# Windowed attention into a gated feed-forward layer: the output layer of five wide tiles as seven block products

## The chip, the cores and the metric

The kernel runs on one core of a Trainium2 chip. A core has a matrix engine (TensorE, PE in the profile), a vector engine (VectorE, DVE), a scalar engine (ScalarE, ACT), a general engine (GpSimd, POOL) and a queue engine (SyncE, SP) that issues transfers. Each engine works off its own instructions in order; semaphores tie them together. The metric is the device time of one execution in microseconds, the median of several runs.

## The reference

Eight batches of eight heads, 576 tokens each, head size 64: causal attention with a window of 64 tokens, then a gated feed-forward layer over all 4608 tokens (model width 512, inner width 1536).

```python
scores = (1.0 / np.sqrt(D)) * np.matmul(q, k.transpose(0, 1, 3, 2))
rel = pos[:, None] - pos[None, :]
scores = np.where((rel >= 0) & (rel < 64), scores, -1000000000.0)
attn = np.exp(scores - max) ; attn = attn / (sum + 1e-09)
x = np.matmul(attn, v)                    # (8, 8, 576, 64) -> (4608, 512)
gate = np.maximum(x @ w_gate, 0.0)        # (4608, 1536)
out = gate * (x @ w_val) @ w_out          # (4608, 512)
```

## The kernel before

**Tiles.** The tokens are cut into four narrow tiles of 384 and six wide tiles of 512. For the wide tiles (here "wide tile 1" to "wide tile 6"; `t` from 4 to 9 in the code) the work of one tile is: attention of the tile, a transposed and normalized input `xt` of 128 partitions by 4 by 512, the inner layer `fast_hidden` (L547), and the output layer `fast_output` (L646). The inner features are 12 blocks of 128.

**The inner layer.** It runs in three groups of two lower and two upper feature blocks. In each group the gate half is four plain products of `xt` with `wg` (L582), passed through a rectifier by ScalarE (L586) into `r4`. The value half is already done as seven block products for eight (Winograd's form of Strassen's method): the products P1, P6, P2, P5, P7, P4, P3 (L573, four matmuls of 256 columns each) use differences of the tokens (`xc`, made by `x_form` on DVE, L459) and differences of the weights (`vs`, made once by `w_form` on POOL, L480). Three running sums in a PSUM bank are copied out by ScalarE (`snap`, L593); DVE adds them to another bank (`vsum`, L600); POOL multiplies such a sum with the rectified gate into `g_sb` (L606). One quarter of a group needs no sum, and DVE multiplies it straight from the bank (L613). So per group there are three sums on DVE, three multiplications on POOL and one on DVE. P3 adds onto the bank that the second sum reads, and therefore comes after it.

**The output layer.** `fast_output` takes the tile's four quarters of 128 tokens in turn: 12 matmuls of 512 columns (L658) with a block of `g_sb` as the stationary operand and `wo` as the moving one, a copy to `o_sb` by ScalarE (L663) and a store of 128 rows by SP's queue (L665). In the last tile the last quarter goes out in three pieces of 256, 128 and 128 columns (`output_last`, L703 to L707).

**What stands between the quarters.** The attention of later tiles is worked into the output layer: `values` of the next tile (L422, 64 small matmuls for each half of the heads) before quarters one and two, `scores` of the tile after that (L253, 64 small matmuls) before quarters three and four. `values` needs three PSUM banks, which DVE's normalizations give back (`t_norm`, L441); `scores` needs four, which ScalarE's exponentials give back (L389). DVE then masks (L394), and `t_turn` (L447) transposes the result into `xt`.

**POOL's queue.** Besides its multiplications POOL issues the loads of queries, keys and values (L173, L199) and copies value rows between partition halves (L208, L210). A query or key load waits until DVE has transposed the batch that is in the buffer (L193).

**The order.** The program is written out by hand. A small planner (`Weaver`) keeps a clock that runs with the matmuls' modelled time and a heap of actions with due times; before each product the actions that are due are written into their engines' streams. What it settles is only the order in each engine; waits come from the data. Eight PSUM banks go round in a list `free`. A pool `g_sb` has two buffers, `r4` two, `vsum` four, `snap` five, `o_sb` three.

## Time and profile before

| | |
|---|---|
| median of 3 runs | 322.14 us (321.91 to 322.75) |
| the profiled execution's own time | 322.06 us |
| its span in the trace | 320.2 us |
| granted clock, mean | 0.995 |
| wide tiles 1 to 6 begin about (first product of the tile) | 122.3, 157.0, 190.0, 223.1, 256.0, 287.4 us |

The profile is of one execution. Times inside it are microseconds from the start of its span. A group's row gives line, engine, operation, output and inputs, shapes and count, then busy time and the mean of one in nanoseconds, then the idle time of the engine just ahead of these instructions and what ended it. A row of the chain or of an engine's instructions in order of time gives start, length, and what ran; "x8" means eight of them merged. Matmuls overlap in the pipeline, so the distance between starts is what one costs, not its own length.

### The profile page before, as it was taken

The numbers are of one execution on the slowest core, as the hardware profiler recorded it, in microseconds if no ns is written. First come the engines' busy times: TensorE is split into PE (matmuls) and PEld (weight loads), VectorE is DVE, ScalarE is ACT, GpSimd is POOL, SyncE is SP. The second block draws the span as 40 slices with busy tenths as digits, with TensorE's granted clock in tenths as the row PEclk, the third lists the DMA queues.
The fourth block names the chain that finished last, engine by engine and source line by source line (L and its number), as shares of the span: only waits on it lengthen the run. The fifth ranks groups of instructions, "written<-read, shape, count | busy, mean of one in ns | idle before, by whom it ended". The sixth has DMA issues, their size and how long they took to land.

```text
span 320.2 us, 9481 instructions
## 1 busy us (share of the span) xinstructions
PE 308.8 (96%) x4077; PEld 190.1 (59%) x4077; DVE 203.2 (63%) x397; ACT 158.1 (49%) x310; POOL 177.8 (56%) x206
## 2 busy tenths in 40 slices
PE   4799999999899999999999999999999999999996
PEld 2586958655546555665566556655665566546654
DVE  6937962667993996779576857686337734643420
ACT  3644325533524616752765276627652666326632
POOL 8859336215988506799168925980495036404540
PEclk9889999999999999999999999999999999999999
DMA  8999998946299149806910691039001100020002
GB/s 218 183 196 205 194 120 161 171 98 99 30 174 165 21 90 160 57 1 104 219 36 0 97 220 43 2 50 127 35 0 34 69 34 3 2 98 35 0 33 102
DMA packets 52491, 29.52 MB, mean 92 GB/s; under 512 B 38880, under 2 KB 43872, under 8 KB 52448
## 3 DMA queue, kind: packets, MB, share of 16 engines
q0 software_dynamic: 46688, 18.29, 49.3%
q1 hardware_dynamic: 5616, 10.55, 9.3%
q8 instruction: 32, 0.52, 0.7%
q14 instruction: 11, 0.09, 0.1%
q10 hardware_dynamic: 144, 0.07, 0.1%
HBM read 37.75 MB, written 9.44 MB: 147 GB/s over the span
## 4 chain that ended last, share of the span: by engine, by line
PE 89%; DVE 3%; ACT 2%; POOL 2%; DMA 2%; issue 1%; DVEq 0%; POOLq 0%
PE bank L658 19%; PE bank L582 19%; PE bank L538 17%; PE bank L573 17%; PE bank L673 10%; PE bank L253 3%; PE bank L422 2%; DVE p L292 2%; DMA v<-in_v_dram 2%; ACT pw L389 1%; PE bank L311 1%; DVE g_sb L525 1%; PE bank L703 1%; POOL v L199 1%; DVE qT L193 0%
## 5 line engine op out<-in xcount | busy, mean ns | idle before, releaser
L606 POOL TENSOR_TENSOR g_sb<-r,vsum 128x512 f16<-128x512 f32 x54 | 68.1, 1276 | 77.7 <-DVE vsum L600 75.7
L600 DVE TENSOR_TENSOR vsum<-bank,snap 128x512 f32<-128x512 f32 x54 | 37.3, 691 | 60.1 <-PE bank L573 36.5
L582 PE MATMUL bank<-xt,wg 128*128 128x512 f16 x288 | 73.9, 379 | 0.0
L658 PE MATMUL bank<-wo,g_sb 128*128 128x512 f16 x276 | 62.9, 380 | 0.0
L586 ACT ACTIVATE r<-bank 128x512 f32<-128x512 f32 x72 | 43.2, 600 | 32.3 <-PE bank L582 32.3
L658 PEld LDWEIGHTS <-g_sb 128*128 128x128 f16 x276 | 25.5, 98 | 28.9
L582 PEld LDWEIGHTS <-wg 128*128 128x128 f16 x288 | 28.2, 98 | 18.6
L525 DVE TENSOR_TENSOR g_sb<-r,bank 128x384 f16<-128x384 f32 x48 | 25.9, 550 | 20.3 <-PE bank L538 18.8
L522 ACT ACTIVATE r<-bank 128x384 f32<-128x384 f32 x48 | 23.7, 496 | 29.4 <-PE bank L538 20.3
L573 PEld LDWEIGHTS <-vs 128*128 128x128 f16 x288 | 28.0, 98 | 15.6 <-issue 1.6
L538 PE MATMUL bank<-xt,wg 128*128 128x192 f16 (+1 forms) x256 | 36.5, 296 | 0.5 <-DVE g_sb L525 0.4
L663 ACT COPY o_sb<-bank 128x512 f32<-128x512 f32 x23 | 13.5, 586 | 45.2 <-PE bank L658 43.2
L593 ACT COPY snap<-bank 128x512 f32<-128x512 f32 x54 | 31.6, 586 | 8.4 <-PE bank L573 8.4
L199 POOL DMA_DIRECT2D v<-in_v_dram x41 | 34.7, 865 | 1.8 <-DMA q<-in_q_dram 1.0
L538 PE MATMUL bank<-xt,wv 128*128 128x192 f16 (+1 forms) x256 | 34.3, 286 | 0.0
L673 PE MATMUL bank<-wo,g_sb 128*128 128x512 f16 x144 | 32.8, 379 | 0.2 <-DVE g_sb L525 0.2
L538 PEld LDWEIGHTS <-wg 128*128 128x128 f16 x256 | 24.3, 102 | 9.8 <-issue 0.9
L573 PE MATMUL bank<-xc,vs 128*128 128x256 f16 x216 | 29.4, 272 | 0.4 <-ACT snap L593 0.4
L208 POOL COPY v<-v 64x512 f16<-64x512 f16 (+1 forms) x22 | 16.1, 732 | 23.7 <-DMA v<-in_v_dram 22.6
L538 PEld LDWEIGHTS <-wv 128*128 128x128 f16 x256 | 22.9, 98 | 8.1
L394 DVE TENSOR_TENSOR pw<-pw,mask 128x512 f16<-128x512 f16 x48 | 20.2, 437 | 11.2 <-ACT pw L389 10.5
L389 ACT ACTIVATE pw<-bank 128x512 f16<-128x512 f32 x48 | 25.9, 608 | 1.5 <-PE bank L253 1.0
(69 smaller groups left out, 358.6 us busy)
## 6 DMA issues: line engine op xcount, KB each, us to landing
out_dram<-o_sb SPq DMA_DIRECT2D x35, 256.0 KB, 3.0
k<-in_k_dram POOLq DMA_DIRECT2D x15, 288.0 KB, 5.3
q<-in_q_dram POOLq DMA_DIRECT2D x15, 288.0 KB, 7.3
v<-in_v_dram POOLq DMA_DIRECT2D x31, 128.0 KB, 8.0
wg<-in_moe_w_gate_dram POOLq DMA_DIRECT2D x6, 256.0 KB, 6.4
wv<-in_moe_w_val_dram POOLq DMA_DIRECT2D x6, 256.0 KB, 8.2
wo<-in_moe_w_out_dram POOLq DMA_DIRECT2D x3, 512.0 KB, 11.9
v<-in_v_dram POOLq DMA_DIRECT2D x10, 64.0 KB, 5.9
```

Source lines behind the costliest of these rows:

```text
L199: nc.gpsimd.dma_start(v16s[b % 2][lo:hi, g, :, 0:64], v[b, :, 64 * g - 64 + lo:64 * g - 64 + hi].rearrange("h p d -> p h d"))
L389: nc.scalar.activation(d["p"][g].rearrange("p n c -> p (n c)"), d["st"][g], ACT.Exp, scale=scale)
L525: nc.vector.tensor_tensor(g_sb[:, f:f + w, c0:c0 + n], part(r_sb), part(h2), MUL)
L538: nc.tensor.matmul(h[:, b * n:b * n + n], wt[:, c, (f + b) * 128:(f + b) * 128 + 128], xt[:, c, c0:c0 + n], start=(c == 0), stop=(c == NC ...
L573: nc.tensor.matmul(at[to][:, HT * i:HT * i + HT], w[:, k, 128 * i:128 * i + 128], x[:, k], start=(first and i == 0 and k == 0), stop=(k == ...
L582: nc.tensor.matmul(to, wg[:, k, 128 * ff:128 * ff + 128], xt[:, k], start=(k == 0), stop=(k == NC - 1))
L586: nc.scalar.activation(r4[:, n], to, ACT.Relu)
L593: nc.scalar.copy(at[name], at["A"])
L600: nc.vector.tensor_tensor(v, at[to], at[name], ADD)
L606: nc.gpsimd.tensor_tensor(gh[:, 2 * j + HF * n:2 * j + HF * n + 2, h], rh[:, 2 * n:2 * n + 2, h], pair(v), MUL)
L658: nc.tensor.matmul(op, g_sb[:, f, 128 * sub:128 * sub + 128], wo[:, f], start=(i == 0), stop=(i == NF - 1))
L673: nc.tensor.matmul(op, g_sb[:, f, bass.ds(sub * 128, 128)], wo[:, f], start=(f == 0), stop=(f == NF - 1))
```

## The change

**The output layer of wide tiles 1 to 5** (`block_output`, in place of `fast_output`) becomes seven block products. The tile's `g_sb` is cut in two ways: lower and upper six feature blocks, first and second 256 tokens. The output weights are cut in lower and upper feature blocks and left and right 256 columns. Each product has 6 feature blocks by 2 token quarters, 12 matmuls of 256 columns, 84 in all where there were 48 of 512. The order is P1, P5, P6, half of P2, P7, the other half of P2, P4, P3, with `values` and `scores` at four places between. Three snapshots by ScalarE, three sums by DVE straight into `o_sb`, and one copy by ScalarE give the four quarters of the result, each 256 tokens by 256 columns. Wide tile 6 keeps the old form.

**The differences.** `wo_form` makes the weight differences `ws` once, 12 operations of 128 by 512 on POOL: six due at 50.5 us and after by the planner's clock, six due in the last narrow tile. `g_form` makes the token differences `s_sb` for each group of each of the five tiles: two on DVE (n = 0, 1) and two on POOL (n = 2, 3). They read what the group's multiplications wrote, so each stands behind these. In the third group of a tile one of POOL's three multiplications (lower features, first tokens) moves to DVE.

**POOL's order.** In wide tile 1 the six later weight differences stand behind the query loads: five ahead of the value loads, one behind them, all ahead of the first multiplication. In wide tiles 1 and 2 the key and query loads of a later batch stand in the third group between the first difference and the second multiplication.

**Even and odd tokens.** A window's 64 query tokens are split as even and odd in place of first and second 32 in `t_pv`, with strided weight loads, and the even ones fill the first half of the tile. A store then goes to every second row of `out`. With block products a store takes two pieces of 256 numbers per partition, in place of one of 512.

**Buffers.** `s_sb` shares the two-buffer pool of `g_sb`. The zeros that the early heating matmuls read lie in `ws` before it is used. The last tile's three last pieces use `o_sb` in place of own buffers.

```diff
@@ t_pv
-                    n = 2 * (QW * qh + i) + s
+                    n = 2 * QW * s + QW * qh + i
...
-                                         quads[qd]["p"][j][:, QW * hh + i, 32 * s:32 * s + 32],
+                                         quads[qd]["p"][j][:, QW * hh + i, s:64:2],
@@ after w_form
+    def wo_form(n, j):
+        f1, f2 = slice(HF + 2 * j, HF + 2 * j + 2), slice(2 * j, 2 * j + 2)
+        c1, c2 = slice(0, DM // 2), slice(DM // 2, DM)
+        b11, b12, b21, b22 = wo[:, f1, c1], wo[:, f1, c2], wo[:, f2, c1], wo[:, f2, c2]
+        to = ws[:, :, 2 * j:2 * j + 2]
+        x, y = ((b12, b11), (b22, to[:, 0]), (b22, b12), (b21, to[:, 1]))[n]
+        nc.gpsimd.tensor_tensor(to[:, n], x, y, SUB)
...
+    def g_form(t, n, j, eng):
...
+        a11, a12, a21, a22 = g_sb[:, f1, h1], g_sb[:, f2, h1], g_sb[:, f1, h2], g_sb[:, f2, h2]
...
+        x, y, op = ((a21, a22, ADD), (to[:, 0], a11, SUB), (a11, a21, SUB), (a12, to[:, 1], SUB))[n]
+        eng.tensor_tensor(to[:, n], x, y, op)
@@ fast_hidden, group
+                    late = t < LAST and j == NF // 4 - 1 and (n, h) == (0, 0)
...
-                        nc.gpsimd.tensor_tensor(gh[...], rh[...], pair(v), MUL)
+                        (nc.vector if late else nc.gpsimd).tensor_tensor(gh[...], rh[...], pair(v), MUL)
...
+            if t < LAST:
+                late = j == NF // 4 - 1
+                W.at(T + 6.2, lambda: g_form(t, 2, j, nc.gpsimd))
+                W.at(T + (7.1 if late else 9.0), lambda: g_form(t, 0, j, nc.vector))
+                W.at(T + (7.2 if late else 9.1), lambda: g_form(t, 1, j, nc.vector))
+                W.at(T + 8.8, lambda: g_form(t, 3, j, nc.gpsimd))
@@ new: block_output
+        forms = {"P1": (g_sb[:, f1, h1], wo[:, f1, c1], [(HF, 1)]), "P2": (g_sb[:, f2, h1], wo[:, f2, c1], [(0, 1)]),
+                 "P3": (s_sb[:, 3], wo[:, f2, c2], ["s", 3]), "P4": (g_sb[:, f2, h2], ws[:, 3], [(0, 0)]),
+                 "P5": (s_sb[:, 0], ws[:, 0], ["s", 0]), "P6": (s_sb[:, 1], ws[:, 1], ["s", 1]),
+                 "P7": (s_sb[:, 2], ws[:, 2], ["s", 2])}
...
+        run(0)
+        product("P1", "A", True)
+        snap("a1")
+        product("P5", "C", True)
+        run(1)
+        product("P6", "A", False)
+        snap("u2")
+        product("P2", "B", True, (0,))
+        run(2)
+        product("P7", "A", False)
+        snap("u3")
+        add(0.9, "C", "u3", False, 0, c2)
+        product("P2", "B", False, (1,))
+        add(0.1, "B", "a1", True, 1, c1)
+        product("P4", "A", False)
+        W.at(W.clock, direct)
+        run(3)
+        while ("summed", "u3") not in at:
+            W.pop()
+        product("P3", "C", False)
+        add(0.1, "C", "u2", True, 1, c2)
@@ output_last
-            o_sb = consts.tile([128, c1 - c0], FP32, name=f"o_last{c0}")
+            o_sb = f_sb.tile([128, DM], FP32, name="o_sb")[:, 0:c1 - c0]
@@ the plan
+        for j in range(NF // 4):
+            for n in range(2):
+                W.at(50.5 + 1.2 * (2 * j + n), lambda n=n, j=j: wo_form(n, j))
...
+                for j in range(NF // 4):
+                    for n in range(2, 4):
+                        W.at(T + 15.0 + 1.2 * (2 * j + n), lambda n=n, j=j: wo_form(n, j))
...
-                fast_output(t, between)
+                block_output(t, between)
```

## The prediction

> **What bounds the kernel now.** I read the page first (busy shares and the chain), then the groups, then one stretch per wide tile, then the queues of TensorE (PE), GpSimd (POOL) and VectorE (DVE) instruction by instruction. Page:
>
> ```profile
> PE 308.8 (96%) x4077; PEld 190.1 (59%) x4077; DVE 203.2 (63%) x397; ACT 158.1 (49%) x310; POOL 177.8 (56%) x206
> ...
> PE 89%; DVE 3%; ACT 2%; POOL 2%; DMA 2%; issue 1%; DVEq 0%; POOLq 0%
> ```
>
> PE is busy 96% of the span and carries 89% of the chain, so a matmul less is time less, as long as nobody makes PE wait. The groups that price the change:
>
> ```profile
> L606 POOL TENSOR_TENSOR g_sb<-r,vsum 128x512 f16<-128x512 f32 x54 | 68.1, 1276 | 77.7 <-DVE vsum L600 75.7
> L600 DVE TENSOR_TENSOR vsum<-bank,snap 128x512 f32<-128x512 f32 x54 | 37.3, 691 | 60.1 <-PE bank L573 36.5
> ```
>
> POOL multiplies the gates (1.28 us each) as DVE's sums arrive (0.69 us), and now has 77.7 us of rest before them. The wide tiles' stretches (columns: length, busy PE, PEld, DVE, ACT, POOL, clock, DMA share, GB/s):
>
> ```profile
> 157.00:190.00 33.00, 33.00 (x437) 19.65 (x436) 23.20 (x43) 18.49 (x33) 22.20 (x24) 1.00 0.66 91
> 190.00:223.10 33.10, 33.10 (x439) 19.80 (x438) 22.84 (x43) 18.49 (x33) 19.96 (x20) 1.00 0.52 68
> 223.10:256.00 32.90, 32.90 (x438) 19.59 (x437) 18.15 (x38) 18.49 (x33) 15.76 (x15) 1.00 0.09 33
> 256.00:287.40 31.40, 31.40 (x310) 18.59 (x308) 15.01 (x30) 14.36 (x25) 11.30 (x9) 1.00 0.09 35
> ```
>
> PE has no gap in wide tiles 2 to 5; POOL is busy 22.2 of 33.0 us in tile 2, so 10.8 us are spare, but only if they fall in the right place. POOL's queue around the first two wide tiles:
>
> ```profile
> 120.70 0.53 POOL L173 DMA_DIRECT2D q<-in_q_dram  x1 [8.26 <-DVE xc L459]
> 122.92 0.53 POOL L173 DMA_DIRECT2D q<-in_q_dram  x1 [1.69 <-DVE xc L459]
> 123.44 4.22 POOL L199 DMA_DIRECT2D v<-in_v_dram  x5
> 129.67 1.31 POOL L606 TENSOR_TENSOR g_sb<-r,vsum 128x512 f16<-128x512 f32 x1 [2.02 <-DVE vsum L600]
> ...
> 162.63 1.27 POOL L606 TENSOR_TENSOR g_sb<-r,vsum 128x512 f16<-128x512 f32 x1 [9.16 <-DVE vsum L600]
> ```
>
> The query loads hold POOL until 123.4 (their buffer is freed by a DVE transpose); only 2.0 us are free before the first gate of wide tile 1. In wide tile 2 the first gate comes 5.64 us after the tile began (157.0).
>
> **What it removes.** From the chain's own steps, matmuls back to back:
>
> ```profile
> 133.81 0.87 PE bank L573 x8
> ...
> 154.46 2.70 PE bank L658 x12
> ...
> 306.98 7.77 PE bank L658 x36
> ```
>
> Eight 256-column matmuls take 0.87 us (0.109 each); 36 of 512 columns 7.77 (0.216 each; the 2.70 for 12 holds a switch, which the new order has as well). A tile's output goes from 48 x 0.216 = 10.36 to 84 x 0.109 = 9.14 us: 1.22 a tile, 6.1 over five, if PE never waits.
>
> **What it adds to POOL.** Weight differences: 12 at about the 1.21 us of the same shape (L480), start to start 1.20. The first six stand beside the value copies at 45 us; POOL idles 9.7 us before those and 8.8 after, so I cost them at nothing (bounds 0 and 1 us, if a value load is late). The other six stand between the query loads and the first gate: five ahead of the five value loads, one after. 123.45 + 5 x 1.20 + 4.25 + 1.20 = 134.9 for the first gate, 5.2 us later than 129.67.
>
> Token differences: two per group on POOL, 6 x 1.20 = 7.2 us a tile, less one multiplication that moves to DVE. Tile 2 then has 8 x 1.26 + 7.2 + value copies 4.8 + query/key loads 2.25 + value loads 4.3 = 28.6 us in 33, in order.
>
> Follow tile 2 from its start T (a tile's group is 6.53 us, the groups end at T+19.6). POOL starts at T+5.64; before it has done the third group's multiplication for the late tokens of the upper features, which P1 reads, it must do 7 multiplications (8.8), 4 differences (4.8) and the copies (4.8): T+24.05. PE wants it 0.63 (values) + 0.87 (two thirds of P1) after the groups: T+21.1. So POOL is 3 us late without any collision. DVE is held too: its first difference of a group reads a product of POOL, and the next group's sum, and with it that group's P3, stands behind it. For the second group POOL's product is done at T+20.3; differences 0.75, sum 0.65, P3 0.45, direct product and last sum 0.8+0.05, the moved multiplication 0.6, two differences 0.7: T+24.3. Behind these DVE has reciprocals 0.3, norms 1.3, transpose 1.1, reciprocals 0.3, x difference 0.35, two norms 0.85 before the second norm that gives back the fourth bank which the next scores need: T+28.5. Then PE's scores 0.68, P7 1.31, half P2 0.65, P4 1.31, scores 0.68, P3 1.31 = 5.94: the tile ends at T+34.45. Tile 2 has the key/query loads in POOL's queue before the product that P2 reads: T+28.75 + 0.25 + 5.94 = 34.95. Against the stretches shown: tile 2 +1.95, tile 3 +1.35, tile 4 +1.55. Tile 5 has no copies, no loads and no scores: the gain shows, 1.3.
>
> Tile 1, by the same walk from 134.9: 8 multiplications 10.1, 5 differences 6.0, copies 4.8, loads 2.25 give 158.05 for P2's product; +0.25 + 5.94 = 164.25 against 157.0: +7.25.
>
> **DVE against POOL.** The added DVE operations (two SBUF inputs) meet POOL's. The row for that:
>
> ```profile
> 148.28 1.29 DVE L459 TENSOR_TENSOR xc<-xt 128x512 f16<-128x512 f16 x1
> ...
> 147.96 1.30 POOL L606 TENSOR_TENSOR g_sb<-r,vsum 128x512 f16<-128x512 f32 x1
> ```
>
> This 0.42 us difference took 1.29 and ended 0.3 after POOL's; the same at 181.21 (0.86). So a meeting cost 0.87 and 0.44; bounds 0 and a whole POOL instruction, 1.27. I take the mean, 0.65. On the chain three such operations meet POOL in a tile (first difference of groups two and three, the moved multiplication): 2.0; POOL itself is pushed back by DVE's pairs about 0.5. So +2.5 in tiles 3 and 4, +3.1 in tile 2 (its x difference meets one too), +0.3 in tile 5 (slack takes the rest), +3.0 in tile 1 (six masks meet the weight differences: half of 6 x 0.35; two pairs 1.4; one meeting 0.6).
>
> The Trainium skill, page "SBUF — State Buffer", section "Who interferes with whom", says that a DVE instruction with two SBUF inputs contends with a GpSimd instruction that reads SBUF, and that the second fully blocks; the 1.29 us row agrees, and by that rule each of the meetings would cost what is left of POOL's instruction, the upper bound of the sum below. The page "GPSIMD Engine Reference", section "4.1 Engine selection", speaks against the placing: two-input elementwise work is VectorE's, GpSimd being about two times slower; here it is 1.21 against 0.42 us, 2.9 times, and with all differences on DVE the sum would lose POOL's 7.2 us a tile and gain 2 us of DVE.
>
> **Small terms.** Values with even and odd tokens apart: strided weight loads; the score loads already step over every second element (L253, 92 ns) and the value loads take 94: nothing, bounds 0 and 0.1 us. Output pieces of 1 KB for 2 KB: the stores' 3.0 us to landing lie beside a tile; only DVE's add waits for a buffer, before work that has slack: nothing. ScalarE: three snapshots and a copy for four copies: nothing. A pause of PE may cost clock: from 14 to 18 us it was granted 0.57, after a stretch in which PE was busy 4.07 of 6 us; bounds 0 and 1.7 us (4 us x 0.43) for each tile; I take nothing, since the matmuls behind a pause wait for POOL again. The end: the last three copies now use the ring of three output buffers, the third after the store of the third quarter: copied at 315.4, landing 3.0 later, 318.4, for 317.44 now: bounds 0 and 0.95; I take 0.5.
>
> **Sum.** 10.25 + 5.05 + 3.85 + 4.05 - 1.0 + 0.5 = +22.7 us. On the profiled execution's 320.2 us span and 1.86 around it (322.06; the median is 322.14, the same to 0.1): 344.8 us.
>
> **The rivals.**
> A, faster: POOL keeps up and 6.1 us come out; less the end's 0.5 that is 316.5 us. For it: POOL's 77.7 us of rest. Against: the rest lies before T+5.64 and in the output, not in the groups. It decides if POOL does the 17 instructions from T+5.64 in 15.5 us in place of 18.4; the shortest rows of each kind (1.26, 1.15, 0.60 and 1.03) give 17.9.
> B, no collisions: the sum with that term at nothing, 7.25 + 1.95 + 1.35 + 1.55 - 1.3 + 0.5 = +11.3: 333.4. For it: four POOL copies beside DVE masks at 104 to 108 us grew by only 0.1 us each.
> C, full collisions: every meeting costs a whole POOL instruction, so tile 1 +13, tiles 2 to 4 +6.2, +5.1, +5.2, tile 5 +0.7, end +0.95: 353.3.
> D, only tile 1 pays: the weight differences delay it by 7.25 and the later tiles gain 1.1 each: 322 + 7.3 - 4.4 + 0.5 = 325.5. It needs POOL to start tiles 2 to 4 earlier than T+5.64, which the sums forbid.
>
> **How the numbers follow.** Forecast (338 to 350) 0.56, B (331 to 338) 0.20, C (350 to 356) 0.15, D 0.04, A 0.04, nothing either way 0.01. Predicted 344.8; from B's low side to C's, 332 to 354, about 8 in 10; the rest is A, D and what is longer still. Under 0.3% (1 us) a measurement of this kernel tells nothing. Faster 0.04, within 0.01, slower 0.95.
>
> **What would show it.** In the new profile: product matmuls with 256 columns at 0.109 us; the first gate multiplication of wide tile 1 near 135 instead of 129.7; a POOL without gaps from there and in tiles 2 to 4 from about 5.6 us in; PE idle in every one of these tiles, at P3 of groups two and three and in P1 or P2, released by POOL's products or DVE's sums; tile lengths near 45, 38, 37, 37 and 30.4 us (34.7, 33.0, 33.1, 32.9, 31.4 now); DVE differences of over 0.8 us. I am wrong if POOL shows gaps in tile 2's groups: then A or D holds.

## The result and the profile after

The changed kernel takes 359.42 us (median; 357.23 to 360.5) against 322.02 us for the kernel before on the same chip: a ratio of 1.115, 95% interval 1.109 to 1.121. The forecast was 344.8 us in a range of 332 to 354: the direction is right, the size is not, and it lies beyond the range.

The profiled execution of the changed kernel has a span of 358.8 us, 38.6 more than before. Its busy row, its chain, and the groups that answer to those shown of before:

```profile
PE 315.1 (88%) x4257; PEld 210.1 (59%) x4257; DVE 252.3 (70%) x447; ACT 158.1 (44%) x310; POOL 222.7 (62%) x243
...
PE 44%; DVE 26%; POOL 20%; DMA 4%; issue 3%; ACT 2%; POOLq 0%; DVEq 0%; ACTq 0%
...
L639 POOL TENSOR_TENSOR g_sb<-r,vsum 128x512 f16<-128x512 f32 x49 | 62.4, 1284 | 67.4 <-DVE vsum L631 66.5
...
L510 DVE TENSOR_TENSOR s_sb<-g_sb 128x512 f16<-128x512 f16 x15 | 20.8, 1388 | 20.2 <-POOL g_sb L639 19.9
```

PE's part of the chain fell from 89% to 44%; DVE and POOL now carry 46%. POOL's idle time ahead of its multiplications is still 67 us (77.7 before), so an idle sum says little about a queue: it lies where nothing needs POOL. The last row is the new work on DVE. The first token difference of a group (two quarters of `g_sb`) takes 1.39 us on average, where the same shape takes 0.42 undisturbed.

The wide tiles' stretches (columns as before: length, busy PE, PEld, DVE, ACT, POOL, granted clock, DMA share, GB/s):

```profile
122.78:169.26 46.48, 36.03 (x537) 24.23 (x536) 38.20 (x59) 21.78 (x41) 40.54 (x41) 0.96 0.68 77
169.26:210.14 40.88, 34.34 (x475) 23.87 (x473) 31.56 (x53) 18.48 (x34) 28.19 (x29) 0.96 0.50 75
210.14:250.97 40.83, 34.24 (x474) 24.05 (x472) 31.62 (x53) 18.50 (x34) 26.14 (x25) 0.96 0.29 37
250.97:290.50 39.53, 33.93 (x475) 24.03 (x473) 26.69 (x49) 18.55 (x34) 21.90 (x20) 0.96 0.09 30
290.50:324.93 34.43, 32.04 (x346) 22.56 (x344) 24.52 (x43) 15.08 (x27) 17.34 (x14) 0.97 0.13 44
```

All five are longer than forecast, and none has the full clock. What holds tile 2, first on DVE, then on POOL, then on PE:

```profile
187.15 0.69 DVE L631 TENSOR_TENSOR vsum<-bank,snap 128x512 f32<-128x512 f32 x1 [0.43 <-PE bank L604]
190.71 1.47 DVE L510 TENSOR_TENSOR s_sb<-g_sb 128x512 f16<-128x512 f16 x1 [2.86 <-POOL g_sb L639]
192.21 0.42 DVE L510 TENSOR_TENSOR s_sb<-s_sb,g_sb 128x512 f16<-128x512 f16 x1
192.55 0.68 DVE L631 TENSOR_TENSOR vsum<-bank,snap 128x512 f32<-128x512 f32 x1
```

```profile
189.41 2.49 POOL L639 TENSOR_TENSOR g_sb<-r,vsum 128x512 f16<-128x512 f32 x2
192.78 1.16 POOL L510 TENSOR_TENSOR s_sb<-g_sb,s_sb 128x512 f16<-128x512 f16 x1 [0.88 <-DVE s_sb L510]
```

```profile
189.89 1.03 PE L613 MATMUL bank<-xt,wg 128*128 128x512 f16 x4
193.29 0.60 PE L604 MATMUL bank<-xt,vs 128*128 128x256 f16 x4 [2.37 <-DVE vsum L631]
...
200.59 0.20 PE L254 MATMUL bank<-qT,kT 32*128 32x64 f16 x2
202.09 0.18 PE L254 MATMUL bank<-qT,kT 32*128 32x64 f16 x1 [1.30 <-DVE xw L442]
202.62 0.72 PE L254 MATMUL bank<-qT,kT 32*128 32x64 f16 x61 [0.34 <-DVE xw L442]
203.28 2.74 PE L735 MATMUL bank<-ws,s_sb 128*128 128x256 f16 x12
...
206.79 1.47 PE L735 MATMUL bank<-ws,g_sb 128*128 128x256 f16 x12
```

DVE waits 2.86 us for POOL's product, the first of the two at 189.41. Then its difference meets the second, which ends at 191.90, and takes 1.47, to 192.18; the sum behind it comes at 192.55, and PE's P3 at 193.29, after 2.37 us of rest. At the scores PE waits for banks that DVE's norms give back, and the twelve matmuls of P7 after that take 2.53 us from start to start, where P4's twelve take 1.41 with the switch. Stretches of PE alone (length, busy PE, clock, DMA share, GB/s) show why: the clock is halved for about three microseconds (203.06 to 206.47, as the section on the clock shows).

```profile
193.30:200.80 7.50, 7.15 (x176) 1.00 0.39 62
203.20:206.00 2.80, 2.80 (x24) 0.50 1.77 177
207.00:210.10 3.10, 3.10 (x88) 1.00 1.62 227
```

### The profile page after: what moved, and what is told of

It is laid out like the page before. It is cut to its first block, busy times and chain, and to the rows that moved or that the text cites. A ratio compares the mean times of both kernels' runs of the same rounds, so it can differ in the third digit from the quotient of the medians.

```text
span 358.8 us, 9985 instructions
## 1 busy us (share of the span) xinstructions
PE 315.1 (88%) x4257; PEld 210.1 (59%) x4257; DVE 252.3 (70%) x447; ACT 158.1 (44%) x310; POOL 222.7 (62%) x243
## 4 chain that ended last, share of the span: by engine, by line
PE 44%; DVE 26%; POOL 20%; DMA 4%; issue 3%; ACT 2%; POOLq 0%; DVEq 0%; ACTq 0%
PE bank L569 12%; DVE s_sb L510 8%; PE bank L604 8%; PE bank L613 7%; PE bank L795 6%; PE bank L735 6%; POOL g_sb L639 5%; POOL s_sb L510 4%; DVE xw L442 4%; DVE xt L448 3%; DMA wg<-in_moe_w_gate_dram 2%; POOL v L211 2%; DVE vsum L631 2%; POOL v L209 2%; PE bank L700 2%
## 5 line engine op out<-in xcount | busy, mean ns | idle before, releaser
L639 POOL TENSOR_TENSOR g_sb<-r,vsum 128x512 f16<-128x512 f32 x49 | 62.4, 1284 | 67.4 <-DVE vsum L631 66.5
L624 ACT COPY snap<-bank 128x512 f32<-128x512 f32 x54 | 31.7, 587 | 27.4 <-PE bank L604 26.7
L613 PEld LDWEIGHTS <-wg 128*128 128x128 f16 x288 | 28.5, 99 | 19.3 <-issue 0.6
L569 PE MATMUL bank<-xt,wg 128*128 128x192 f16 (+1 forms) x256 | 35.2, 286 | 1.6 <-DMA wg<-in_moe_w_gate_dram 0.8
L510 DVE TENSOR_TENSOR s_sb<-g_sb 128x512 f16<-128x512 f16 x15 | 20.8, 1388 | 20.2 <-POOL g_sb L639 19.9
L795 PE MATMUL bank<-wo,g_sb 128*128 128x512 f16 x144 | 32.8, 379 | 0.2 <-DVE g_sb L556 0.2
L390 ACT ACTIVATE pw<-bank 128x512 f16<-128x512 f32 x48 | 26.8, 605 | 12.3 <-PE bank L254 12.1
L395 DVE TENSOR_TENSOR pw<-pw,mask 128x512 f16<-128x512 f16 x48 | 25.3, 536 | 7.8 <-ACT pw L390 7.6
L604 PE MATMUL bank<-xt,vs 128*128 128x256 f16 x72 | 11.6, 287 | 20.3 <-DVE vsum L631 20.3
L569 PEld LDWEIGHTS <-wg 128*128 128x128 f16 x256 | 22.8, 98 | 11.1 <-DMA wg<-in_moe_w_gate_dram 1.4
L735 PEld LDWEIGHTS <-s_sb 128*128 128x128 f16 x240 | 23.7, 104 | 9.3 <-issue 2.6
L745 ACT COPY snap<-bank 128x512 f32<-128x512 f32 x15 | 8.8, 588 | 42.2 <-PE bank L735 40.7
```

Of the source, the lines that this page charges most:

```text
L390: nc.scalar.activation(d["p"][g].rearrange("p n c -> p (n c)"), d["st"][g], ACT.Exp, scale=scale)
L510: eng.tensor_tensor(to[:, n], x, y, op)
L569: nc.tensor.matmul(h[:, b * n:b * n + n], wt[:, c, (f + b) * 128:(f + b) * 128 + 128], xt[:, c, c0:c0 + n], start=(c == 0), stop=(c == NC ...
L604: nc.tensor.matmul(at[to][:, HT * i:HT * i + HT], w[:, k, 128 * i:128 * i + 128], x[:, k], start=(first and i == 0 and k == 0), stop=(k == ...
L613: nc.tensor.matmul(to, wg[:, k, 128 * ff:128 * ff + 128], xt[:, k], start=(k == 0), stop=(k == NC - 1))
L624: nc.scalar.copy(at[name], at["A"])
```

## The experiments

All were compared with the kernel before on the same chip. Tile lengths are read from the profiles, from the first product of a wide tile to the first of the next.

| kernel | median us | ratio, 95% | tile 1 | 2 | 3 | 4 | 5 |
|---|---|---|---|---|---|---|---|
| before | 322.02 | | 34.72 | 33.02 | 32.91 | 32.87 | 31.42 |
| forecast | 344.8 | | 45 | 38 | 37 | 37 | 30.4 |
| changed | 359.42 | 1.115 (1.109 to 1.121) | 46.48 | 40.88 | 40.83 | 39.53 | 34.43 |
| one_input | 346.38 | 1.075 (1.073 to 1.078) | 44.83 | 38.39 | 35.75 | 37.01 | 32.36 |
| diffs_only | 349.66 | 1.085 (1.083 to 1.087) | 45.22 | 37.99 | 37.86 | 38.66 | 31.42 |
| diffs_dve | 353.72 | 1.099 (1.095 to 1.102) | 46.72 | 40.31 | 38.29 | 37.20 | 32.76 |
| diffs_pool | 374.12 | 1.161 (1.158 to 1.164) | 51.72 | 43.40 | 44.22 | 41.64 | 35.89 |
| pool_order | 341.75 | 1.062 (1.058 to 1.065) | 39.33 | 38.06 | 35.44 | 37.26 | 34.68 |
| both_orders | 337.65 | 1.050 (1.046 to 1.054) | 38.99 | 35.41 | 35.21 | 35.18 | 34.87 |
| both_one | 332.99 | 1.033 (1.032 to 1.035) | 39.14 | 36.35 | 33.55 | 33.55 | 33.21 |
| no_diffs_gap | 322.70 | 1.001 (0.999 to 1.003) | 35.36 | 33.94 | 31.96 | 31.92 | 31.03 |

**Where the weight differences stand.** Two other places for the six later ones: among the narrow tiles, at about 58 to 65 us (ws_early), and between the key and the query loads at 113 to 121 us, where POOL waits for DVE anyhow (ws_gap).

```diff
 ws_early, beside the first six:
+            for n in range(2, 4):
+                W.at(64.2 + 0.1 * (2 * j + n), lambda n=n, j=j: wo_form(n, j))
 ws_gap, the query loads of that batch 0.3 us later in the order and the differences between:
-                        W.at(T + 15.0 + 1.2 * (2 * j + n), ...)
+                        W.at(T + 15.7 + 0.01 * (2 * j + n), ...)
```

> The six later weight differences moved from before wide tile 1 to about 58 to 65 us of the trace, where POOL rests; all else as in the changed kernel. If POOL's queue is what makes tile 1 long, the first gate multiplication comes back to about 129.7 us and tile 1 shrinks from 46.5 to about 38 to 39 us: 351 us in all. If the collisions of DVE with POOL are what counts, the eight masks of the start fall from 1.3 to 0.42 us but the tile shrinks by no more than some 3 us: 356 us. If the work is only pushed elsewhere (value copies at 65 us late), nothing is gained: 359 us.

> As the changed kernel, but the six later weight differences stand between the key loads and the query loads at 112 to 121 us, where POOL waits 8 us for DVE's transposes and DVE runs no operation with two inputs in SBUF. If the cost of ws_early in the narrow tiles (wide tile 1 began 9.2 us later) came from its place beside DVE's masks, wide tile 1 begins at 122 to 123 us as before and is 42 to 43 us long: 355 us. If any place costs the same, 359 us again.

ws_early took 361.45 us (1.121, 1.116 to 1.126): tile 1 is 4.2 us shorter, but begins 9.2 us later. The twenty-four masks of the narrow tiles (L293) met POOL and grew from 0.53 us (11.9 in sum) to 0.87, and PE waited for them; 10.2 us at half clock behind these waits (65.0 to 75.2) are part of the delay:

```profile
PEld L312 <- DVE p L293: 6.3, 9, 1.7
...
PE bank L312 <- DVE p L293: 4.9, 6, 1.6
```

ws_gap took 353.69 us (1.099, 1.096 to 1.102), 5.7 less than the changed kernel: tile 1 begins at 122.69, as in the changed kernel (122.78), and is 42.33 us long. So the placing of six weight differences before the first gate costs 4 to 6 us, of the 7.25 that were forecast.

**Who makes the token differences.** All four on DVE, or all four on POOL:

```diff
 diffs_dve
-                W.at(T + 6.2, lambda: g_form(t, 2, j, nc.gpsimd))
+                W.at(T + 6.2, lambda: g_form(t, 2, j, nc.vector))
-                W.at(T + 8.8, lambda: g_form(t, 3, j, nc.gpsimd))
+                W.at(T + 8.8, lambda: g_form(t, 3, j, nc.vector))
 diffs_pool: nc.gpsimd for nc.vector in n = 0 and 1
```

> All four differences of a group on DVE, none on POOL; weight differences as in the changed kernel. POOL loses 7.2 us a tile, DVE gains six operations of 0.34 us, or of up to 1.6 us when they meet POOL. If POOL's queue is the bound, tiles 2 to 4 lose 3 us or more each: 345 us or less. If DVE's collisions with POOL are the bound, the six added ones eat it: 356 to 365 us.

> All four differences of a group on POOL, none on DVE; weight differences as in the changed kernel. DVE no longer waits for POOL's products and meets POOL less. If POOL's queue is the bound, each tile gets 7.2 us more of it, less 2 to 3 of collisions: tiles 2 to 4 longer by 4 us, 372 to 380 us. If DVE waiting on POOL in front of the next group's sum is the bound, it is faster: 345 to 355 us.

With all on DVE the time falls by 5.7 us, to between the two ranges expected; with all on POOL it rises by 14.7. With the differences on POOL none of DVE's is left to meet it, and the queue is the bound by itself: P1 waits 7.73 to 7.75 us for POOL's product in each of tiles 1 to 4. A waits' row of that kernel (sum, times, longest):

```profile
PE bank L735 <- POOL g_sb L639: 34.4, 6, 7.8
```

**The wait in DVE's order.** The DVE differences of groups one and two, and POOL's last, 3.3 and 3.7 us later in the order, so that the next sum goes ahead of them:

```diff
-                W.at(T + (7.1 if late else 9.0), lambda: g_form(t, 0, j, nc.vector))
+                W.at(T + (7.1 if late else 12.3), lambda: g_form(t, 0, j, nc.vector))
-                W.at(T + (7.2 if late else 9.1), lambda: g_form(t, 1, j, nc.vector))
+                W.at(T + (7.2 if late else 12.4), lambda: g_form(t, 1, j, nc.vector))
-                W.at(T + 8.8, lambda: g_form(t, 3, j, nc.gpsimd))
+                W.at(T + (8.8 if late else 12.5), lambda: g_form(t, 3, j, nc.gpsimd))
```

> As the changed kernel, but DVE's two token differences of groups one and two of a tile (and the last one of POOL, which reads them) come 3.3 us later in the order, behind the next group's second sum in place of in front of it. If DVE standing before a product of POOL holds the next sum, and P3 with it, the two pauses of about 2.2 and 2.4 us before P3 go: tiles 2 to 4 fall from 40 to 41 to about 36 to 37 us, 342 to 346 us in all. If POOL's queue itself sets the end of the tile, P1 and P2 wait in place of P3 and the tiles stay at 39 to 41 us, 355 us or more.

356.44 us (1.107, 1.104 to 1.110): only 3 us less. The pauses before P3 of tile 2 are gone, and PE stands at P1 and P5 in their place:

```profile
192.11 0.61 PE L735 MATMUL bank<-wo,g_sb 128*128 128x256 f16 x4 [2.25 <-POOL g_sb L639]
...
195.52 1.03 PE L735 MATMUL bank<-ws,s_sb 128*128 128x256 f16 x4 [1.44 <-DVE s_sb L510]
```

The wait moved; POOL's queue sets the end of the groups, as the prediction's sum of seven multiplications, four differences and the copies said (P1 2.25 us late, 3 forecast).

**Meetings of the differences taken away.** DVE's differences read one SBUF operand in place of two, at the same place in the order and behind the same product.

```diff
-        eng.tensor_tensor(to[:, n], x, y, op)
+        if eng is nc.vector:
+            for i in range(2):
+                nc.vector.transpose(to[:, n, i], x[:, i] if n == 0 else a11[:, i])
+        else:
+            eng.tensor_tensor(to[:, n], x, y, op)
```

> The changed kernel with VectorE's token differences replaced by two transposes of 256 each of one of the operands: one SBUF input in place of two, same place in the order, same wait for the product. The differences' values are left out, so the result is not the reference's. If the meeting of two-input VectorE work with GpSimd is what lengthens the groups, the L510 operations end at their own length (about 0.35 us a piece, none near 1.3), the pauses before P3 of groups two and three fall from 2.2 us to under 1.3, the half clock at the scores goes, and tiles 2 to 4 take 36 to 37.5 us in place of 39.5 to 40.9: about 345 us (340 to 350). If the wait for GpSimd's product in VectorE's order is what costs, whatever the operation behind it, the pauses stay near 2 us and the time above 355 us.

346.38 us, 13.0 less than the changed kernel. The replaced operations take 0.41 us each and at most 0.45, two of them for one difference. Other meetings stay: the masks of the wide tiles (0.56 us on average, 0.55 in the changed kernel) and the moved multiplication (1.19, 1.05 there).

```profile
L512 DVE STREAM_TRANSPOSE s_sb<-g_sb 128x256 f16<-128x256 f16 x60 | 21.7, 412 | 10.1 <-POOL g_sb L643 10.1
```

PE no longer rests before P3 in tiles 2 to 4, nor at the scores; it waits at P1 for POOL, 3.68, 3.23 and 3.30 us (the forecast walk without meetings had 3.0). One thing that was expected did not come: the halved clock stayed, now behind the pause at P1 in tiles 2 and 4, and not in tile 3.

```profile
192.62 1.03 PE L739 MATMUL bank<-wo,g_sb 128*128 128x256 f16 x4 [3.68 <-POOL g_sb L643]
193.45 2.77 PE L739 MATMUL bank<-ws,s_sb 128*128 128x256 f16 x12
```

```profile
192.60:198.00 5.40, 5.38 (x85) 0.50 0.58 85
...
230.60:241.60 11.00, 10.82 (x268) 1.00 0.92 78
```

**Making against using.** All differences made, the output layer as before and nothing reading them; and the opposite, block products that read quarters of `g_sb` with no token differences (the result is then another), with the weight differences at the narrow tiles' place (no_diffs) or at that of ws_gap (no_diffs_gap).

```diff
 diffs_only
-            if t == LAST:
+            if t < LAST:
+                fast_output(t, between)
+            elif t == LAST:
                 fast_output(t, between[:-1])
                 W.drain()
 ...
 no_diffs, no_diffs_gap: the four g_form lines out; in block_output
-                 "P3": (s_sb[:, 3], wo[:, f2, c2], ["s", 3]), ...
+                 "P3": (g_sb[:, f2, h1], wo[:, f2, c2], [(0, 1)]), ...   (P5, P6, P7 alike)
```

> The changed kernel with all its differences made at their places, but the output layer of tiles 1 to 5 as before, four times twelve matmuls of 512 columns; the differences are not read. It tells the cost of making them from the cost of the products that wait for them. If making them is what costs (groups held by VectorE's sums, wide tile 1 delayed by the weight differences), the pauses before P3 of groups two and three stay at 2.2 us, tile 1 takes 45 to 47 us and tiles 2 to 4 38 to 41: 352 to 360 us. If the output's products waiting for differences, banks and the half clock behind them cost most, tiles 2 to 4 fall to 36 to 37.5 us: 342 to 350 us.

> As ws_early, but with no token differences at all: P3, P5, P6 and P7 read quarters of the gates in their place, so the output is not the reference's; what is left out is these 60 operations. Matmuls, sums, stores and order of the output layer stay. If the differences (POOL's queue and DVE's waits on it) are the cause, the 6.1 us of matmuls appear: 316 to 318 us and tile lengths near 31.9 us. If the block products themselves (banks, sums on DVE before P3, smaller stores) cost, it stays above 322 us.

> As no_diffs (no token differences; P3, P5, P6, P7 read quarters of the gates, so the output is not the reference's), but with the later weight differences between the key and query loads as in ws_gap, so that the narrow tiles are undisturbed. What the block products are worth when nothing waits for a difference: 6.1 us by the matmuls alone, 316 us; tiles 1 and 2 of no_diffs lost 1.4 and 1.5 us at scores to a wait that the trace puts down to nothing, which would leave 318 to 321 us.

diffs_only took 349.66 us: the making alone costs 27.4, most of it in the groups. Tile 5 is then 31.42 us, exactly as before, since nobody waits for its differences. The block products on top cost another 9.8 us, where the forecast had them gain 6.1. With neither token differences nor a bad place (no_diffs_gap) the time is 322.70 us, that of before: tiles 3 and 4 gain 0.95 us each, near the 1.22 of the arithmetic, tiles 1 and 2 lose 0.64 and 0.92, at the scores, behind a wait for which the view names no releaser:

```profile
155.29 0.58 PE L254 MATMUL bank<-qT,kT 32*128 32x64 f16 x52
157.27 0.27 PE L254 MATMUL bank<-qT,kT 32*128 32x64 f16 x12 [1.40 <-issue]
```

Waits of this kind over 0.7 us stand in eight of the kernels, eleven in all, and always before one of two matmuls, PE's 2270th or 2654th. The trace's list of transfers has a queue for instructions (q8) with pieces of 16 KB: 33 of them for the 8514 matmuls and weight loads of the changed kernel, some 258 each. The two matmuls are 768 matmuls and weight loads apart, about three pieces, and each time the 17th or the 20th piece lands 1.25 to 1.6 us before PE goes on (here at 155.75, PE at 157.27). That points to the loading of PE's own program; no run moves it, so it is argued and not shown.

no_diffs took 329.82 us (1.023, 1.018 to 1.028), with tile 1 beginning 8.5 us late. So in this order nothing was to be had: even free differences bring the kernel only back to where it was, 322.70 us, above the 318 to 321 expected.

**Even and odd tokens alone**, put into the kernel before, with the stores to every second row (not printed):

```diff
-                    n = 2 * (QW * qh + i) + s
+                    n = 2 * QW * s + QW * qh + i
-        quads[qd]["p"][j][:, QW * hh + i, 32 * s:32 * s + 32],
+        quads[qd]["p"][j][:, QW * hh + i, s:64:2],
```

> The kernel before with one part of the change alone: a window's tokens split as even and odd, with strided weight loads in the value products and stores to every second row. The prediction has this at nothing: 322.0 us, within 0.3%. If the strided loads or stores cost, up to 0.5 us a wide tile: 325 us.

322.13 us, ratio 1.000 (0.999 to 1.002): the part costs nothing.

**The clock.** Dead matmuls in the pauses, eight of 512 columns before P3 of groups two and three (heat), seven before the scores (heat_scores); and pauses made in the kernel before, by four DVE fills before the last sum of groups two and three in tiles 2 to 5.

```diff
 heat, before P3 (heat_scores: seven, before the third attention block of the output)
+            if t < LAST and j > 0:
+                to = bank()
+                for _ in range(8):
+                    nc.tensor.matmul(to, ident, wo[:, 0], start=True, stop=True, skip_group_check=True)
+                free.insert(0, to)
 pause_before, on the kernel before, ahead of vsum
+                    if (n, h) == (1, 1) and j > 0 and NS < t < LAST:
+                        for _ in range(4):
+                            nc.vector.memset(dead, 0.0)
```

> As the changed kernel, with eight dead matmuls (128 by 512, 1.7 us) into a free bank before P3 of groups two and three of wide tiles 1 to 5, where PE otherwise pauses 2.2 to 4 us. If the halved clock after the pauses (7 to 8 us of clock in sum) lies on the path, each tile with pauses gets 1.2 to 1.7 us shorter: 352 to 354 us. If the matmuls behind a pause wait for POOL and DVE anyway, as the prediction had it, 359 us or, in tile 5, where there is no pause in the groups, 3.4 us more.

> As the changed kernel, with seven dead matmuls (1.5 us) before the scores between P2's halves, where PE waits 1.3 to 1.7 us for a bank. If the halved clock of P7 in tiles 2 and 3 (2.5 us for 1.3) comes from that wait, the clock stays and tiles 2 to 4 get 1 to 1.5 us shorter: 355 to 357 us. If the clock falls for another reason, the same as the changed kernel or up to 1 us longer: 359 to 361 us.

> The kernel before with four VectorE fills of 128x512 (some 0.5 us each) ahead of the last sum of groups two and three in wide tiles 2 to 5: it makes PE pause about 1.5 to 2.2 us before P3 twice a tile, without any GpSimd work. It prices pauses by themselves. If a pause of about 2 us costs only its own length, the tiles grow by 3 to 4.4 us, the clock stays at 1.00 and the time is 334 to 340 us. If pauses of this length halve the clock for some 2.5 us each, the tiles' clock falls to about 0.95 and the tiles grow by another 1 to 2.5 us each: 339 to 350 us.

heat took 362.81 us (1.127, 1.124 to 1.129) and heat_scores 358.05 (1.111, 1.109 to 1.113). In heat PE rests only 0.43 to 0.64 us before P3 of groups two and three in tiles 2 and 3, and the clock is halved all the same, at the scores. So the pauses before P3 are not its cause there: 1.31 and 0.35 us at the scores are enough. In heat_scores the clock drops elsewhere in the tiles. The price by itself neither settles. The rows of heat, PE in time and then PE's clock behind the scores (the length, busy PE, PEld, DVE, ACT, POOL, clock, DMA share, GB/s):

```profile
202.83 0.18 PE L254 MATMUL bank<-qT,kT 32*128 32x64 f16 x1 [1.31 <-DVE xw L442]
203.36 1.01 PE L254 MATMUL bank<-qT,kT 32*128 32x64 f16 x61 [0.35 <-DVE xw L442]
204.30 2.65 PE L740 MATMUL bank<-ws,s_sb 128*128 128x256 f16 x12
```

```profile
203.90:206.60 2.70, 2.70 (x47) 1.95 (x36) 2.70 (x6) 1.57 (x3) 2.50 (x4) 0.50 1.71 180
```

pause_before took 325.87 us (1.012, 1.010 to 1.013): DVE's slack took up most of the fills, one pause of 1.18 us was left in each of tiles 2 and 3, and the clock stayed at 1.00 in every tile. So a pause of 1.2 us alone cost no clock here. The longer pauses that were meant did not come about, and longer ones were not tried by themselves.

What decides can be read from the traces of all 18 kernels together. Every half-clock stretch that ends inside a program is 3.41 us long, or two or three times that, and within one execution all of them begin on one grid of 3.41 us. Call a step of this grid a window. For the work in a window, take each matmul's columns at 0.42 ns (512 cost 0.216 us) times the part of the 128 by 128 array that it uses (a score matmul 32 of the rows, a value matmul 32 of the columns), and divide the sum by 3.41 us. From 20 us on, 44 windows at full clock had a share of work under 0.34, and all 44 were followed by a window at half clock; of 12 with 0.34 to 0.376 it was 10; of 1561 with more, none. (In the first 15 us this does not hold: there were such windows without half clock behind them.) So it is not the length of a pause alone that counts, but how little work is left in one window. In diffs_only a pause of 2.32 us before P3 lies in one window (share 0.27), with no other wait near it; in one_input, tile 3, a pause of 3.23 us is cut in two by a border (0.41 and 0.50), and the clock stays whole (columns: length, busy PE, clock, DMA share, GB/s):

```profile
180.21:183.62 3.41, 1.09 (x7) 1.00 0.00 0
183.62:187.03 3.41, 3.41 (x14) 0.50 0.00 0
187.03:190.44 3.41, 3.41 (x26) 1.00 0.00 0
```

```profile
225.48:228.89 3.41, 1.85 (x75) 1.00 0.02 5
228.89:232.30 3.41, 1.74 (x16) 1.00 0.00 0
232.30:235.71 3.41, 3.41 (x136) 1.00 0.02 5
```

The grid lies differently in each execution (its first border is at 0.66 us in the kernel before, at 1.68 in the changed one), so which pauses will cost clock cannot be told ahead.

**Better orders.** pool_order has the weight differences of ws_gap, DVE's differences as in due_later, and POOL's six token differences behind its last multiplication, with the key and query loads between. both_orders also has the products as P1, P2, P5, P6, P7, P4, P3, and the first scores behind P7. both_one is that with the one-input operations.

```diff
 pool_order
-                W.at(T + 6.2, lambda: g_form(t, 2, j, nc.gpsimd))
-                W.at(T + 8.8, lambda: g_form(t, 3, j, nc.gpsimd))
+                for k in range(NF // 4 if late else 0):
+                    W.at(T + 8.1, lambda k=k: g_form(t, 2, k, nc.gpsimd))
+                    W.at(T + 8.3, lambda k=k: g_form(t, 3, k, nc.gpsimd))
 both_orders, after P1
-        product("P5", "C", True)
+        product("P2", "B", True)
+        add(0.1, "B", "a1", True, 1, c1)
         run(1)
+        product("P5", "C", True)
         product("P6", "A", False)
 ...
```

> All work of the change, in another order: later weight differences as in ws_gap; DVE's differences of groups one and two as in due_later; POOL's six differences of a tile behind its last multiplication, the key and query loads between them. If POOL's in-order queue is what made the products late, P1 no longer waits and tiles 1 to 4 fall from 40 to 46 to 34 to 36 us: 326 to 330 us. If DVE's collisions with POOL at the end of the tile (3 to 4 us) are the larger part, the tiles stay at 36 to 38 us: 334 to 340 us.

> As pool_order, and the output layer's products in the order P1, P2, P5, P6, P7, P4, P3, with the scores behind P7 in place of between P2's halves: P5 then comes 1.3 us later for DVE's differences, and the scores' banks are free. If the wait for banks at the scores and the halved clock behind it are worth what the trace shows (1.7 and 1.3 us a tile), tiles 1 to 4 are 32 to 33.5 us: 320 to 324 us. If a wait takes their place, no better than pool_order.

> The kernel with both orders changed (337.65 us) and the same one-input operations in place of VectorE's differences. If what is left there is again the meetings, the pauses before P5 and P3 (0.7 and 1.2 us) mostly go and tiles 2 to 4 take 33.5 to 34.3 us in place of 35.3: about 333 us (330 to 335). If what is left comes from the order of the banks and the sums, nothing moves: 336.5 to 338.5 us. In neither case is it below 322 us, since wide tile 1 keeps some 4 us of its own.

341.75, 337.65 and 332.99 us; pool_order is slower than both of its ranges, both_orders far from its 320 to 324 us. The order alone takes 21.8 of the 37.4 us back. In both_orders no pause of tiles 2 to 4 is over 1.4 us and the clock is 1.00 throughout:

```profile
197.26:232.47 35.21, 32.25 (x474) 23.27 (x472) 31.01 (x53) 18.34 (x33) 27.94 (x27) 1.00 0.53 59
```

What is left in these tiles is a row of small waits (from PE's rows of tile 3):

```profile
220.34 0.61 PE L736 MATMUL bank<-wo,g_sb 128*128 128x256 f16 x4 [0.38 <-POOL g_sb L639]
...
222.33 2.78 PE L736 MATMUL bank<-ws,s_sb 128*128 128x256 f16 x24 [0.70 <-DVE xw L442]
225.78 1.47 PE L736 MATMUL bank<-ws,s_sb 128*128 128x256 f16 x12 [0.67 <-ACT snap L746]
...
231.16 1.47 PE L736 MATMUL bank<-wo,s_sb 128*128 128x256 f16 x12 [1.15 <-DVE o_sb L752]
```

Without the differences' meetings (both_one) the first of these falls to 0.21, the wait for the norms goes, and that for DVE's output sum falls to 0.42: 1.66 us a tile in tiles 3 and 4. Tile 2 is 0.94 us longer: a half-clock stretch lies at its start (160.9 to 164.3), behind a wait of 2.87 us of the kind for which no releaser is named. Nothing that was run beats the kernel before.

## Why the prediction was wrong in size

**What held.** The first gate multiplication of tile 1 stands at 135.62 us (forecast 134.9, before 129.67), POOL starts 5.64 us into tile 2 and then rests only twice in its groups (0.89 and 0.88 us, for DVE's differences; 0.5 in sum was forecast), 256-column matmuls cost 0.110 us, the even and odd tokens nothing. The last tile grew by 0.87 us (33.87 for 33.0, some 0.5 of it the halved clock at its start) for 0.5. The mechanism is the forecast one: POOL's queue late for P1 and holding DVE, DVE's order holding P3 and the fourth bank. POOL's lateness at P1 shows only where P3 no longer waits: 3.2 to 3.7 us in one_input, for 3.0. POOL's rest of 77.7 us was rightly not taken for room.

The prediction's sum can be laid beside the runs. The clock is taken out as an estimate: half of the time that PE spent in half-clock stretches, on the chain and in all.

| term | forecast us | measured us | from |
|---|---|---|---|
| walks without clock, and the end | +11.3 | +17 to +18 | one_input 346.4, less 322.3 and its clock; the masks and the moved multiplication still meet POOL in it |
| meetings of DVE and POOL | +11.4 | +13 | changed less one_input: the token differences' meetings alone |
| halved clock | 0 | +6 to +7 | one_input: 5.9 on the chain, 6.8 in all (changed kernel: 5.6 and 8.5) |
| sum over 322.1 | +22.7 | +37 | changed less before: +37.4 |

**The failed steps: the gain "if PE never waits", and "I take nothing" for the clock.** The 6.1 us of the products stand whole in the sum; without them it has 28.8 us for the making of the differences and what waits for it. Making them without using them cost 27.4 (diffs_only; about 5 of it clock on its chain, which the 28.8 has not, so the agreement is partly luck). The products, put at -6.1, cost 9.8 on top: a swing of 15.9 us, more than the whole miss of 14.6. Both kernels lost about as much clock (9.0 and 8.5 us), so this part is not the clock's. What the runs show in place of the gain is PE waiting: by length less busy time it idles 10.5, 6.5, 6.6, 5.6 and 2.4 us in tiles 1 to 5 of the changed kernel, and 7.4, 3.2, 3.1, 3.8 and 0.0 in diffs_only.

For the clock the prediction named the cost (bounds 0 and 1.7 us a tile) and took its low end, "since the matmuls behind a pause wait for POOL again". The trace of the changed kernel has five half-clock windows in the wide tiles, from 141.6, 203.1, 244.0, 274.7 and 322.5 us: one in each of tiles 1 to 4, and one over the end of tile 5 and the start of tile 6. At 1.7 us each that is 8.5 us, the named upper bound. The reason held for two: in tile 1 the chain runs over POOL at that time, in tile 4 mostly over DVE. It fails for the other three: the slow matmuls are P7 and P2 in tiles 2 and 3 and P3 in tile 5, where POOL's work for the tile is over and the output is PE's own chain. Along the chain 5.6 us are lost. The nearest to a test is in one_input: behind waits of 3.23 and 3.30 us at P1, tile 3 ends 11.07 us later at full clock (241.63) and tile 4 12.34 us later with one half-clock window (278.64), 1.27 more:

```profile
230.56 0.61 PE L739 MATMUL bank<-wo,g_sb 128*128 128x256 f16 x4 [3.23 <-POOL g_sb L643]
...
266.30 0.93 PE L739 MATMUL bank<-wo,g_sb 128*128 128x256 f16 x4 [3.30 <-POOL g_sb L643]
```

How much of the miss is the clock's stays open all the same. No run changes it alone; both_orders, where it is 1.00, changes the waits as well. And the four executions of the changed kernel lost 8.6, 10.4, 12.1 and 13.6 us of clock (one less the granted clock, times the span) and took 360.50, 359.28, 357.23 and 359.56 us: more lost clock was not more time.

The Trainium skill, page "TensorE: Matmul & The Clock Gate", section "Part 1: The HAM clock gate (the "warmup" mystery)", puts the half clock behind an idle window of about 3.4 us that runs free of the program. The traces agree on the window and its free run. They differ on the idling: a window need not be idle, one with a share of work under 0.34 was always enough from 20 us on. So pauses of 2.32 us (diffs_only, share 0.27) or of 1.31 and 0.35 us beside small matmuls (heat, 0.32) cost clock, where one of 1.36 (both_orders, 0.50), one of 1.18 (pause_before, 0.61) and one of 3.23 us cut in two did not.

**The meetings: a sum near the forecast by luck, wrong in size by piece.** The mean of 0.65 us a meeting was taken from two rows as if the phase were chance. It isn't. DVE's first difference is released by the end of a POOL multiplication, and POOL begins its next instruction at that moment, ahead of it: so nearly every one waits a whole POOL instruction, and the group's mean is 1.39 us against 0.42, near 1 us more, with 1.48 and 1.47 in tile 2. The sum came to 13 for 11.4 although it leaves out meetings that the 11.4 had (the masks of tile 1, the moved multiplication), and by tile it is 1.7, 2.5, 5.1, 2.5 and 2.1 for 3.0, 3.1, 2.5, 2.5 and 0.3. Part of that is where the clock fell: tile 3 has a half-clock window in the changed kernel and none in one_input, tile 2 one against two. The Trainium skill's rule ("SBUF — State Buffer", "Who interferes with whom"), by which the second of the two blocks until the first is done, is what these rows show, and the two transposes with one input, never over their own length, are its other half.

**The walks.** Taking 1.7 us for each half-clock window out of one_input, tile 2 is 35.0 us (forecast without meetings 34.95), tile 4 35.3 (34.45), tile 3 35.75 (34.45), tile 1 43.1 (41.97). The worst is tile 5, with no half clock: 32.4 for 30.1. "Tile 5 has no copies, no loads and no scores: the gain shows", and in the small terms "only DVE's add waits for a buffer, before work that has slack: nothing", left out that P3 adds onto the bank that a DVE sum must read first, and that this sum stands behind DVE's norms, transposes and `xc` for tile 6:

```profile
319.16 1.25 DVE L448 STREAM_TRANSPOSE xt<-xw 128x1024 f16<-128x1024 f16 x1
320.44 0.43 DVE L460 TENSOR_TENSOR xc<-xt,xc 128x512 f16<-128x512 f16 x1
320.78 0.69 DVE L751 TENSOR_TENSOR o_sb<-bank,snap 128x512 f32<-128x512 f32 x1
321.38 0.42 DVE L460 TENSOR_TENSOR xc<-xt 128x512 f16<-128x512 f16 x1
321.72 0.69 DVE L751 TENSOR_TENSOR o_sb<-bank,snap 128x512 f32<-128x512 f32 x1
```

```profile
322.46 2.68 PE L735 MATMUL bank<-wo,s_sb 128*128 128x256 f16 x12 [2.28 <-DVE o_sb L751]
```

PE's P3 waits 2.28 us for it and then runs at half clock (2.47 us for 1.32); in one_input it waits 1.60. Before, ScalarE's copies emptied the bank, and PE had no gap in this tile. In the group the prediction had this very dependence (sum before P3) written down; it was not carried over to the output.

**The gain.** The 6.1 us that stood in the sum do not exist as a whole even with free differences: 322.70 for 322.06 in no_diffs_gap. 1.9 us are seen in tiles 3 and 4, tile 5 gives 0.4, tiles 1 and 2 lose 1.6, and tile 1 begins 1.2 us later. In the changed kernel PE's busy time over the five tiles, with the half-clock windows taken at full speed, is 162.9 us for 164.2: 1.3 less, as far as modelled ends tell.

**The rivals.** A and D fell by the tile lengths: tiles 2 to 4 are 6.7 to 7.9 us longer than before. The sign that the prediction named for them, gaps of POOL in tile 2's groups, did come (0.89 and 0.88 us), but they are POOL waiting for DVE and no room: the sign was badly chosen. B, no meetings, is nearest to one_input: 346.4 us, not 333.4. C, full meetings (353.3), had the size of a meeting right, but more of them than were measured (about 19 us for 13), and no clock. What stays open: the wait called "issue" at the scores of tiles 1 and 2 (0.7 to 2.9 us), for which PE's instruction transfers are the candidate, and how much of the lost clock is lost time.

## What to carry to other kernels

Before an engine is given more work because it idles, write its queue and the queues that wait for it out in order, and carry every "reads before it is written" bank into the new code: a sum that moves from an idle engine to a busy one brings that engine's backlog with it. If one engine's two-input work is released by another engine's instruction, price the meeting at a whole instruction, not at an average phase. A gain that stands "if the matrix engine never waits" belongs into the sum only for the tiles in which the walk has it not waiting. Where a change makes the matrix engine pause, put a clock term into the sum and the range: here 1.7 us behind each window of 3.41 us in which it had less than about 0.37 of its full work, on the path only where nothing waits behind it.

## What was not expected of the hardware

Two half-length transposes with one SBUF input took less time beside a busy GpSimd (0.82 us) than one difference with two (1.39). The clock was halved behind 1.31 and 0.35 us of waiting at the scores (heat), and stayed whole behind 3.23 us in another kernel, since the share of work in a window of 3.41 us, on a grid that runs free of the program, decided. And PE waited 1.4 to 1.8 us in blocks of 64 small matmuls (L254, tiles 1 and 2 of no_diffs_gap) with no engine named: each time a 16 KB piece of PE's instructions had landed 1.5 us before it went on.
